# A planned DeltaNet and Fourier-mix kernel: every order drawn anew on a changed plan, integer additions on GpSimd in halves, second table loaded in four

## The chip, the cores and the metric

The kernel runs on one core of a Trainium2 chip. The metric is the device time of one execution in microseconds (us); the time before is the median of three runs.

## The reference: what is computed

For each of 4 batches and 8 heads, the first block walks through 768 tokens of width 48 with a 48x48 state (DeltaNet). The second block takes the heads joined to rows of 384, adds the real part of a Fourier transform over tokens and features, normalises each row and applies a two-layer MLP with 1536 hidden columns.

```python
for t in range(S):
    kt, vt, bt = k_n[:, :, t], v[:, :, t], beta[:, :, t, None]
    y[:, :, t] = einsum('bhd,bhde->bhe', q[:, :, t], state)
    v_old = einsum('bhde,bhd->bhe', state, kt)
    state = state + bt[..., None] * einsum('bhd,bhe->bhde', kt, vt - v_old)
...
u = x + real(fft(fft(x, axis=1), axis=2))
un = (u - mean(u)) / sqrt(var(u) + 1e-6)
out = u + maximum(un @ w_ch1, 0) @ w_ch2
```

The two weight matrices arrive as 64-bit floats. The kernel makes 32-bit floats of them with integer operations.

## The kernel before, in words

**Units and rounds.** Each batch is cut into 6 units of 128 tokens, 24 units in all. Units are prepared in rounds: round 0 has 2, round 1 has 4 (these six are batch 0), and six later rounds have 3 each (`SIZES`). Preparing a unit means loading its k, q and v, turning k and q on TensorE against the identity (L565), forming blocks of k times k (`keys`, `gram`), and inverting triangular blocks on VectorE. Rounds 0 and 1 invert in `begin16`/`invert16` (L897 transposes, L957/L963 multiply and add), later ones in `begin`/`invert` (L853, L868, L1046/L1051, L1063). A chain of state steps then runs through the units of a batch, `chain0` for batch 0 and `step` for the others.

**Mixing and MLP.** When a batch's last unit is done, `mixing` folds its rows on VectorE (L1451), multiplies by the sine and cosine tables `tab` (batch 0 with the first table, later batches with a smaller second one, both in the same tile) and `ft`, normalises (L1604 to L1629), and runs the MLP (L562 with `R`, `w` names, ReLU in L1695). Matmuls all go through the helper at L562, turns through L565, evictions mostly through L571 (ScalarE) or L573/L575 (VectorE).

**Weights.** `weights` brings the two matrices in 18 pieces of 128x512. For each piece: two DMAs or four into a stage buffer (L613), a ScalarE absolute value (L2015), a VectorE clamp (L2018), a ScalarE scaled copy of the low words (L2021), a VectorE shift (L2026), one GpSimd integer addition of 512 columns (L2031), and a VectorE step that puts the sign back (L2034) and needs the addition.

**What sets the order.** Every operation above is entered in a `Plan` with a cost for each engine that may run it, what it reads and writes, a priority and for some a due time. `Plan.schedule` walks a modelled clock and picks for each engine what to start next; `Plan.issue` then writes the instructions out in just that order, so the order on each engine, the DMA queue SP included, is fixed at build time. It rests on:

- due times of the batches and of the MLP: `M00`, `M0`, `MP`, `MX`, `MN`, `MA`, `MT`, `MD` (used in `due_a`, `due_m`, `normed`), and offsets `IV`, `IV1` (inversions) and `WP` (weights). Due times go back from each operation to what it needs. The smallest `pr` goes first;
- `KEYS`: for each 64 operations a number that shifts their priorities by up to 2.5 either way (`shift`);
- `LIM`, `LIM2`: how many of the 8 PSUM banks each class of work may hold before and after `TSW`;
- `START`, `LATER`: settings of the picking rule before and after `TSW`;
- the port rule: while GpSimd is in an operation marked `port=True`, no VectorE operation so marked is started, and the other way round;
- a model of transfers: 0.45 for an issue, `RATE` 190 KB/us, 2 us to land;
- a model of the fetch of TensorE's instructions (`fetch`: `LAND`, `LAND2`, `HOLDUP` and others) and of TensorE's clock (`speed`: costs are doubled while a window of `WIN` 3.413 us has held too few columns).

**Filler matmuls.** Where TensorE has nothing to start, the plan puts matmuls whose result nobody reads (`idle`). Before `E2` = 5.0 one filler is a group of six small ones (L2265), later it is one 256-column matmul or two half-size ones (L2272). In addition, between 20 and `D1` fillers go ahead of ordinary work whenever the last `SPANW` us held fewer than `TARGET` columns per us (`light`). `Plan.issue` writes a filler that starts before 1.5 three times (`OPEN` = 3).

**Hot operations.** `P.hot` marks operations that TensorE's picking rule (`pick`) takes ahead of all else when the mark is 1, and that are only spared by some filters when it is 2. Before, `chain0` has 2 (`HOTC`).

Of the kernel before, what the change touches and what calls it, by code (L numbers as in the profile page):

```python
# [10 lines left out]
I32 = mybir.dt.int32  # L11
U32 = mybir.dt.uint32
AX = mybir.AxisListType
ALU = mybir.AluOpType
# [4 lines left out]


SHIFT, PART = 5.0, 64
KEYS = [0, 196, 0, 882, 0, 533, 747, 349, 300, 92, 0, 631, 0, 118, 229, 329, 112, 81, 189, 0, 488, 857, 205, 426, 209, 734, 514, 433, 0, 264, 416, 0, 634, 135, 91, 0, 140, 556, 752, 279, 934, 886, 297, 564, 670, 480, 0, 737]
SIZES = 3, 3, 3, 3, 3, 3


# [7 lines left out]
class Op:  # L33
# [3 lines left out]

RATE = 190.0
WIN, WARM, COLD, CLOCK = 3.413, 600.0, 560.0, True
LOOK, EARLY = 1e9, 0.6403  # L40
FOLD, BY, SEQ, HOT, HOTPE, HOTPK, HOTG, NORM = 1, 1, 10, 5.6131, 8, 12, 1, 1
HOTC, PORT, E2, OPEN = 2, 1, 5.0, 3
GAP, HALF = 0.2477, 85.6671
LATE = -63.0868
PLOOK, PHOLD, PEND = 0.9458, 0.292, 163.9053
NHALF = 1
FORCE = -320.3215
BLOCK, LEAD, SEEK, LAND, LAND2, HOLDUP = 256, 60, 1.0, 2.0432, 1.8604, 1.0
PACE, PGAP, MOVED = 6.0, -0.4268, -0.7
PACED, AHEAD, SOON = 6.0, 1.6, 0.8  # L50
CUT, ROW = 256, 121
PLAIN, W1T = {(2, 2): (0, 1, 2, 3, 4, 5), (3, 2): (4, 5)}, 0.112
WF = 2, 2
TARGET, SPANW = 768.6683, 4.0822
E0, E1, D1 = 1.0, 10.0, 266.9663
TSW = 120.3811
# [6 lines left out]
LATER = {"SHARE": 0.4509, "HOLD": 0.168, "GAP2": 0.4292, "WAIT": 6.0709, "GATHER": 3.3164, "URGENT": -23.9166,  # L63
         "FIRST": 57.7347, "EV": 17.9188, "STAY": 0.2508, "CHAIN": 1.0}
START = {"SHARE": -0.4066, "HOLD": 0.343, "GAP2": 1.1196, "WAIT": 12.1835, "GATHER": 0.967, "URGENT": -81.5401,
         "FIRST": -86.5298, "EV": 4.7125, "STAY": 0.0, "CHAIN": 0.0}
LIM2 = {"state": 1, "sum": 4, "attn": 11, "mix": 4, "mlp": 4, "norm": 3, "win": 19}


T_F3, T_F2, T_PAIR = 0.36, 0.32, 0.52  # L70
# [3 lines left out]
class Plan:  # L74
# [116 lines left out]
    def schedule(self, pick, limits, switch, idle=None, span=()):  # L191
# [18 lines left out]
        moved, landed = MOVED, [0.0] * 8  # L210
# [9 lines left out]
        done, n, now = 0, len(ops), 0.0  # L220
        order, strict, last, self.hold = [], True, None, False
        self.order = order
        while done < n:
# [4 lines left out]
            for e in self.ENG:  # L228
                if free[e] > now + 1e-9:
                    continue  # L230
                best = None
# [8 lines left out]
                if e == "PE":  # L240
# [29 lines left out]
                    if (best is None and not low and now >= span[0][0] and  # L270
                            not any(o.ready["PE"] < now + (GAP if inside else K["GAP2"])
                                    for o in avail["PE"] if room(o))):
                        low = True
                    two = None
                    if low and best is None and idle:
                        m = "64" if mode == "64" and now < HALF else "128"
                        two = self.spare(now, m)
                    if two:
                        best = Op()
                        best.mode = m  # L280
                        best.i, best.fn, best.deps = -1, idle(two, m, now), set()
                        best.pr, best.lat, best.due, best.kb, best.col = 0.0, 0.0, 0.0, 0, 1150 if now < E2 else 512
                        best.ni = 24 if now < E2 else 8 if m == "64" else 4
                        best.engs, best.new, best.banks, best.succ = {"PE": 0.65 if now < E2 else 0.432}, [], [], []
                        for s in two:
                            slots[s] = now + 0.43
                elif cand:
# [20 lines left out]
                o = best  # L308
# [154 lines left out]
def kernel(  # L463
# [93 lines left out]
    def I(x):  # L557
        kp(x)
        P.ins = x.ins
# [23 lines left out]
    def t_pool(n):  # L583
        return 0.20 + n * 1.9e-3
# [25 lines left out]
    def dma(o, i, wr, pr, rd=(), kb=200, q="SP", cut=()):  # L610
        def fn(e):
            for x in cut or (slice(None),):
                I((nc.sync if q == "SP" else nc.scalar).dma_start(out=o[x], in_=i[x]))  # L613
        P.op({q: 0.45}, fn, rd, wr, pr, lat=2.0, kb=kb)

# [1367 lines left out]
    def weights(src, dst, rows, cols, where, pr, pieces=None):  # L1983
# [10 lines left out]
        for c0 in pieces:  # L1994
# [34 lines left out]
            def f4(e, cc=cc, rr=rr):  # L2029
                w = cc.bitcast(I32)  # L2030
                I(nc.gpsimd.tensor_tensor(w, w, rr.bitcast(I32), op=ALU.add))  # L2031

            def f6(e, cc=cc, hi=hi, c0=c0):
                I(nc.vector.scalar_tensor_tensor(  # L2034
# [223 lines left out]
    def idle(two, mode, now):  # L2258

        w = pack if now > E1 else p_[0]  # L2260

        def fn(e):
            if now < E2:
                for i in range(6):
                    I(nc.tensor.matmul(pst[two[0]][0:64, 64 * i:64 * i + 64], lhsT=w[:, 0:64],  # L2265
                                       rhs=w[:, 64:128], start=True, stop=True,
                                       skip_group_check=True))
                return
            for i in range(2 if mode == "64" else 1):
                x = slice(64 * i, 64 * i + 64) if mode == "64" else slice(0, 128)  # L2270
                n = 64 if mode == "64" else 128
                I(nc.tensor.matmul(pst[two[0]][x, 0:256], lhsT=w[x, 0:n], rhs=w[x, 0:256],  # L2272
                                   start=True, stop=True, skip_group_check=True))
        return fn
# [36 lines left out]
```

## Time and profile before

| what | value |
|---|---|
| median of three runs | 636.96 us (636.93 to 637.67) |
| the profiled execution | 636.25 us, span 634.4 us |
| TensorE busy (matmuls) | 616.8 us, 97% |
| VectorE busy | 512.4 us, 81% |
| ScalarE busy | 269.2 us, 42% |
| GpSimd busy | 35.9 us, 6% |
| instructions | 23099 |
| data moved by DMA | 32.02 MB |

The span runs from the first instruction to the last; the profiled execution's time is 1.85 us more. The tables of the profile name engines PE (TensorE), PEld (its weight loads), DVE (VectorE), ACT (ScalarE), POOL (GpSimd), SP (SyncE, here the queue of transfers). A name ending in q is the engine's sequencer. In a row of the timeline the first number is the start, the second the length, in us, and in brackets is how long the engine stood idle and who ended that; in the chain of waits the second number is the time that the step cost the chain. "Busy" counts any time with a matmul in flight, also when few columns flow, and it counts fillers.

### The profile page before, as it was taken

Reading aid. Unit: us, or ns where it says so; the run is one execution under the profiler, and the core shown is the slowest. Engines: PE = TensorE matmul, PEld = TensorE weight load, DVE = VectorE, ACT = ScalarE, POOL = GpSimd, SP = SyncE. Lnnn points to the kernel's source line nnn. Section 1 sums busy time; section 2 is a strip of 40 time slices with the busy share of each in tenths; the row PEclk is TensorE's granted clock in tenths of the full one; section 3 lists DMA queues with packets and bytes.
Section 4 is the critical chain, followed back from the end, with each engine's and each line's share of the span. In section 5 each row is a group of like instructions: output and inputs, shape, how many; then the busy total and the mean of one; then the engine's idle time right before and its main releaser. Section 6 shows DMA issues by size and latency. Waiting matters only on the chain.

```text
span 634.4 us, 23099 instructions
## 1 busy us (share of the span) xinstructions
PE 616.8 (97%) x9924; PEld 505.2 (80%) x9924; DVE 512.4 (81%) x1524; ACT 269.2 (42%) x791; POOL 35.9 (6%) x42
## 2 busy tenths in 40 slices
PE   8999899999899999999999999999999999999998
PEld 7788888777678777777787788677777889999997
DVE  6999899999995799999945999999666463856573
ACT  5698667531347533425364254253441141322110
POOL 3104311320000000000000000000000000000000
PEclk9999999999999999999999999999999999999999
DMA  8765565300124220001321200000000000000000
GB/s 168 191 193 130 136 134 157 100 3 25 26 42 104 41 53 2 25 3 34 83 54 39 65 14 1 25 3 2 5 28 2 0 26 1 26 1 27 1 26 26
DMA packets 85440, 32.02 MB, mean 50 GB/s; under 512 B 75992, under 2 KB 80825, under 8 KB 85337
## 3 DMA queue, kind: packets, MB, share of 16 engines
q1 hardware_dynamic: 85145, 30.31, 19.3%
q8 instruction: 78, 1.28, 0.8%
q10 hardware_dynamic: 192, 0.23, 0.1%
q14 instruction: 25, 0.20, 0.1%
HBM read 25.81 MB, written 4.72 MB: 48 GB/s over the span
## 4 chain that ended last, share of the span: by engine, by line
PE 73%; DVE 20%; ACT 3%; issue 3%; DMA 1%; DVEq 0%; SPq 0%; ACTq 0%
PE pp L562 69%; DVE tmp L1046 3%; DVE rr L1051 3%; PE pp L565 3%; ACT us L571 1%; DVE w L2034 1%; PE pp L2265 1%; DVE w L2018 1%; DVE gd L807 1%; PE pp L2272 1%; DVE R L1451 1%; DVE us L784 1%; DVE rr L897 1%; DVE rr L853 1%; DVE tmp L957 1%
## 5 line engine op out<-in xcount | busy, mean ns | idle before, releaser
L562 PE MATMUL pp<-R,w 128*128 128x256 f32 (+1 forms) x832 | 182.6, 367 | 0.2 <-DVE us L784 0.2
L562 PEld LDWEIGHTS pp<-R,w 128*128 128x128 f32 x832 | 145.2, 190 | 19.3 <-issue 0.4
L562 PE MATMUL pp<-w,R 128*128 128x384 f32 x384 | 134.8, 494 | 0.0
L571 ACT ACTIVATE us<-pp 32x128 f32<-32x128 f32 (+3 forms) x240 | 75.8, 348 | 80.6 <-PE pp L562 61.1
L562 PEld LDWEIGHTS pp<-w,R 128*128 128x128 f32 x384 | 69.9, 190 | 40.7 <-issue 0.2
L562 PE MATMUL pp<-us 64*64 64x64 f32 (+4 forms) x2784 | 68.4, 229 | 3.1 <-issue 1.6
L1695 ACT ACTIVATE R<-pp 128x512 f32<-128x512 f32 x48 | 28.7, 597 | 98.2 <-PE pp L562 87.6
L562 PEld LDWEIGHTS pp<-us 64*64 64x64 f32 (+2 forms) x2784 | 57.5, 131 | 9.2 <-issue 3.5
L1046 DVE TENSOR_TENSOR tmp<-rr 128x30 f32<-128x30 f32 (+9 forms) x180 | 57.7, 328 | 2.0
L1051 DVE TENSOR_TENSOR rr<-rr,tmp 128x108 f32<-128x108 f32 (+9 forms) x180 | 56.6, 323 | 2.0
L562 PEld LDWEIGHTS pp<-u,us 64*64 64x64 f32 (+1 forms) x1472 | 36.2, 130 | 15.8 <-issue 8.2
L562 PE MATMUL pp<-u,us 64*64 64x48 f32 (+2 forms) x1472 | 42.2, 216 | 0.9 <-DVE mv L573 0.6
L1870 DVE TENSOR_TENSOR us<-us,pp 128x256 f32<-128x256 f32 x64 | 26.7, 419 | 12.1 <-ACT us L571 9.8
L571 ACT ACTIVATE R<-pp 128x192 f32<-128x192 f32 (+6 forms) x82 | 22.8, 336 | 31.6 <-PE pp L565 19.6
L1360 DVE TENSOR_TENSOR u<-u,pp 64x192 f32<-64x192 f32 x66 | 22.3, 349 | 17.1 <-PE pp L562 14.9
L1826 DVE TENSOR_TENSOR gd<-us 128x128 f32<-128x128 f32 x48 | 11.8, 288 | 23.4 <-ACT us L1902 15.2
L571 ACT ACTIVATE x<-pp 64x192 f32<-64x192 f32 (+1 forms) x78 | 24.0, 322 | 14.9 <-PE pp L562 12.4
L562 PE MATMUL pp<-st,us 48*64 48x48 f32 (+1 forms) x1232 | 28.1, 221 | 2.0 <-DVE tmp L1046 0.7
L562 PEld LDWEIGHTS pp<-st,us 48*64 48x64 f32 x1232 | 23.7, 134 | 7.6 <-issue 3.9
L571 ACT ACTIVATE u<-pp 64x192 f32<-64x192 f32 (+1 forms) x71 | 23.1, 326 | 13.3 <-PE pp L562 8.9
L562 PE MATMUL pp<-us,gd 128*128 128x192 f32 x144 | 27.8, 327 | 0.0
L1426 DVE TENSOR_TENSOR x<-x,pp 64x192 f32<-64x192 f32 x66 | 23.2, 352 | 4.6 <-PE pp L562 2.8
(173 smaller groups left out, 959.5 us busy)
## 6 DMA issues: line engine op xcount, KB each, us to landing
out_dram<-x SPq DMA_DIRECT2D x11, 384.0 KB
us<-in_k_dram SPq DMA_DIRECT2D x16, 192.0 KB
us<-in_q_dram SPq DMA_DIRECT2D x16, 192.0 KB
us<-in_v_dram SPq DMA_DIRECT2D x16, 192.0 KB
x<-in_moe_w_ch_dram SPq DMA_DIRECT2D x12, 242.0 KB
R<-in_moe_w_ch_dram SPq DMA_DIRECT2D x6, 256.0 KB
us<-in_k_dram SPq DMA_DIRECT2D x8, 181.5 KB
us<-in_v_dram SPq DMA_DIRECT2D x8, 181.5 KB
```

Source lines behind the costliest of these rows:

```text
L562: I(nc.tensor.matmul(o, lhsT=lhsT, rhs=rhs, start=start, stop=stop, skip_group_check=True))
L565: I(nc.tensor.matmul(o, lhsT=src, rhs=ident[p0:p0 + n, p0:p0 + n], is_transpose=True, start=start, stop=True, skip_group_check=True))
L571: I(nc.scalar.activation(o, i, ACT.Copy, **({} if scale is None else {"scale": scale})))
L784: I(nc.vector.tensor_tensor(z.LT.rearrange(hs, s=2)[:, s], bk()[:, 0], m_su[:, None, :].broadcast_to([128, NJ, 64]), op=ALU.mult))
L807: I(nc.vector.scalar_tensor_tensor(w[0], w[1], (m1, m0)[s], w[2], op0=ALU.mult, op1=ALU.add))
L1046: I(eng(e).tensor_tensor(T_, R[:, :, j + 1:32, j:j + 1].broadcast_to([128, ns, n, j]), R[:, :, j:j + 1, 0:j].broadcast_to([128, ns, n, j]) ...
L1051: I(eng(e).tensor_tensor(R[:, :, j + 1:32, 0:j], R[:, :, j + 1:32, 0:j], T_, op=ALU.add))
L1360: I(nc.vector.tensor_tensor(U[:, s], U[:, s], psum(b1[s])[a, s0:s1].rearrange("p (j d) -> p j d", d=D), op=ALU.subtract))
L1426: I(nc.vector.tensor_tensor(w, w, v, op=ALU.add))
L1695: I(nc.scalar.activation(o, s, ACT.Relu))
L1826: vec(128, lambda e, j=j, i0=i0, i1=i1, op=op: I(nc.vector.tensor_tensor(s(j), i0, i1, op=op)), [aH] + rd, [aS(j)], pr - P.ev)
L1870: vec(256, lambda e: I(nc.vector.tensor_tensor(o, i0(), i1(), op=ALU.add)), [], [aH] + list(wr), pr - P.ev, use=n)
```

## The change

The code changes in seven places, and all of the plan's numbers are replaced.

1. **Opening.** The threefold writing of the first filler is gone. Until the modelled time 5.3 (`OPEN`) TensorE is given fillers alone, from 1.0 on, each a group of six at a cost of 0.7 (doubled while the modelled clock is low). The later kind of filler is counted as 600 columns, not 512.
2. **Transfers.** A transfer's landing after 16 us is planned 1.0 us later (`SLACK`). An issue costs 0.75 for over 50 KB and 0.3 for less.
3. **Integer additions.** L2031 becomes two of 256 columns.
4. **Second table.** Its one DMA of 641 KB becomes four column blocks.
5. **`HOTC`** goes from 2 to 1, `HOTG` from 1 to 7 (the last pair of normalised rows gets the mark too).
6. **Forced fillers.** `TARGET` goes from 768.7 columns per us over 4.08 us to 110.2 over 1.55 us, `D1` from 267 to 157.
7. **Due times, keys, bank limits, fetch times** are all new, so the order on every engine is another.

```diff
-KEYS = [0, 196, 0, 882, ...]
+KEYS = [5, 715, 997, 791, ...]
-WIN ... LOOK, EARLY = 1e9, 0.6403
+LOOK, EARLY = 1e9, -56.6693
-HOTC, PORT, E2, OPEN = 2, 1, 5.0, 3
+HOTC, PORT, E2 = 1, 1, 5.0
-BLOCK, LEAD, SEEK, LAND, LAND2, HOLDUP = 256, 60, 1.0, 2.0432, 1.8604, 1.0
+BLOCK, LEAD, SEEK, LAND, LAND2, HOLDUP = 256, 60, 1.0, 2.2969, 1.7353, 1.0
+OPEN, SLACK = 5.3, 1.0
-TARGET, SPANW = 768.6683, 4.0822
+TARGET, SPANW = 110.1955, 1.5494
-E0, E1, D1 = 1.0, 10.0, 266.9663
+E0, E1, D1 = 1.0, 10.0, 156.9524
-LIM = {"state": 1, "sum": 15, "attn": 6, "mix": 15, "mlp": 11, "norm": 8, "win": 4}
-NW, IV, IV1, WP = 9, 7.4111, 10.4756, -12.4024
-M00 = 96.1793
-M0, MP, MX, MN, MA, MT, MD = 80.4991, 115.1443, 13.2967, 35.8474, 19.0779, 5.7128, 8.8744
+LIM = {"state": 1, "sum": 36, "attn": 12, "mix": 6, "mlp": 16, "norm": 2, "win": 4}
+NW, IV, IV1, WP = 8, 10.1887, 18.6311, -4.1803
+M00 = 69.1361
+M0, MP, MX, MN, MA, MT, MD = 68.5709, 117.666, 17.0826, 39.7315, 19.3597, 6.0685, 9.8539
...
+                    if now < OPEN:
+                        best, low, wait = None, now >= E0, True
...
-                    landed.append(moved + o.lat - (SOON if now < 4.0 else 0.0))
+                    landed.append(moved + o.lat + (SLACK if now > 16.0 else -SOON if now < 4.0 else 0.0))
...
-            for _ in range(OPEN if o.i < 0 and o.start < E0 + 0.5 else 1):
-                o.fn(o.eng)
+            o.fn(o.eng)
...
-        P.op({q: 0.45}, fn, rd, wr, pr, lat=2.0, kb=kb)
+        P.op({q: 0.75 if kb > 50 else 0.3}, fn, rd, wr, pr, lat=2.0, kb=kb)
...
-            P.op({"POOL": t_pool(n) + 0.2}, f4, [a0], [ac], pr, lat=LP, port=True)
+            for h in (0, n // 2):
+                ...
+                P.op({"POOL": 0.73}, f4(h), [A(w0[0], w0[1] + 2 * h, w0[1] + 2 * h + n)],
+                     [A(dst, c0 + h, c0 + h + n // 2)], pr, lat=LP, port=True)
...
-    dma(tab[:, 0:20 * (N6 - 1) + 2], cn["tab6"].ap(), [A(tab, 0, 1)], 0, kb=656)
+    quart = 5 * (N6 - 1)
+    for x in range(4):
+        c = slice(quart * x, quart * (x + 1) + (2 if x == 3 else 0))
+        dma(tab[:, c], cn["tab6"].ap()[:, c], [A(tab, 0, 1, 32 * x, 32 * x + 32)], 0, kb=164)
```

More of the change, by code (lines that the diff above doesn't have):

```diff
@@ L39 @@
 WIN, WARM, COLD, CLOCK = 3.413, 600.0, 560.0, True
-LOOK, EARLY = 1e9, 0.6403
-FOLD, BY, SEQ, HOT, HOTPE, HOTPK, HOTG, NORM = 1, 1, 10, 5.6131, 8, 12, 1, 1
-HOTC, PORT, E2, OPEN = 2, 1, 5.0, 3
-GAP, HALF = 0.2477, 85.6671
-LATE = -63.0868
-PLOOK, PHOLD, PEND = 0.9458, 0.292, 163.9053
-NHALF = 1
-FORCE = -320.3215
-BLOCK, LEAD, SEEK, LAND, LAND2, HOLDUP = 256, 60, 1.0, 2.0432, 1.8604, 1.0
-PACE, PGAP, MOVED = 6.0, -0.4268, -0.7
-PACED, AHEAD, SOON = 6.0, 1.6, 0.8
+LOOK, EARLY = 1e9, -56.6693
+FOLD, BY, SEQ, HOT, HOTPE, HOTPK, HOTG, NORM = 1, 1, 12, 5.5524, 5, 13, 7, 1
+HOTC, PORT, E2 = 1, 1, 5.0
+GAP, HALF = 0.2162, 60.2432
+LATE = -132.6752
+PLOOK, PHOLD, PEND = -5.6692, 0.308, 137.4887
+NHALF = 1
+FORCE = -2.3955
+BLOCK, LEAD, SEEK, LAND, LAND2, HOLDUP = 256, 60, 1.0, 2.2969, 1.7353, 1.0
+PACE, PGAP, MOVED = 6.0, -0.4266, -0.7
+PACED, AHEAD, SOON = 6.0, 1.0, 0.8
+OPEN, SLACK = 5.3, 1.0
 CUT, ROW = 256, 121
@@ L53 @@
 WF = 2, 2
-TARGET, SPANW = 768.6683, 4.0822
-E0, E1, D1 = 1.0, 10.0, 266.9663
-TSW = 120.3811
-LIM = {"state": 1, "sum": 15, "attn": 6, "mix": 15, "mlp": 11, "norm": 8, "win": 4}
-NW, IV, IV1, WP = 9, 7.4111, 10.4756, -12.4024
-M00 = 96.1793
-M0, MP, MX, MN, MA, MT, MD = 80.4991, 115.1443, 13.2967, 35.8474, 19.0779, 5.7128, 8.8744
[L63 to L67, printed above, removed]
+TARGET, SPANW = 110.1955, 1.5494
+E0, E1, D1 = 1.0, 10.0, 156.9524
+TSW = 120.835
+LIM = {"state": 1, "sum": 36, "attn": 12, "mix": 6, "mlp": 16, "norm": 2, "win": 4}
+NW, IV, IV1, WP = 8, 10.1887, 18.6311, -4.1803
+M00 = 69.1361
+M0, MP, MX, MN, MA, MT, MD = 68.5709, 117.666, 17.0826, 39.7315, 19.3597, 6.0685, 9.8539
+LATER = {"SHARE": 0.4054, "HOLD": 0.163, "GAP2": 0.4686, "WAIT": 4.4142, "GATHER": 1.0248, "URGENT": -28.396,
+         "FIRST": 57.2003, "EV": 19.1605, "STAY": 0.1775, "CHAIN": 1.0}
+START = {"SHARE": -0.3965, "HOLD": 0.332, "GAP2": 0.3371, "WAIT": 38.0349, "GATHER": 1.1976, "URGENT": -53.5033,
+         "FIRST": -126.5871, "EV": 8.6017, "STAY": 0.0, "CHAIN": 0.0}
+LIM2 = {"state": 1, "sum": 4, "attn": 17, "mix": 5, "mlp": 6, "norm": 5, "win": 18}
 T_F3, T_F2, T_PAIR = 0.36, 0.32, 0.52
@@ L281, in schedule @@
                         best.i, best.fn, best.deps = -1, idle(two, m, now), set()
-                        best.pr, best.lat, best.due, best.kb, best.col = 0.0, 0.0, 0.0, 0, 1150 if now < E2 else 512
-                        best.ni = 24 if now < E2 else 8 if m == "64" else 4
-                        best.engs, best.new, best.banks, best.succ = {"PE": 0.65 if now < E2 else 0.432}, [], [], []
+                        best.pr, best.lat, best.due, best.kb, best.col = 0.0, 0.0, 0.0, 0, 1010 if now < OPEN else 600
+                        best.ni = 24 if now < OPEN else 8 if m == "64" else 4
+                        best.engs, best.new, best.banks, best.succ = {"PE": 0.7 if now < OPEN else 0.432}, [], [], []
                         for s in two:
@@ L2027, in f3, with f4 @@
                                           op1=ALU.logical_shift_right))
-            def f4(e, cc=cc, rr=rr):
-                w = cc.bitcast(I32)
-                I(nc.gpsimd.tensor_tensor(w, w, rr.bitcast(I32), op=ALU.add))
+            def f4(h, cc=cc, rr=rr):
+                w, r = cc[:, h:h + n // 2].bitcast(I32), rr[:, h:h + n // 2].bitcast(I32)
+                return lambda e: I(nc.gpsimd.tensor_tensor(w, w, r, op=ALU.add))
             def f6(e, cc=cc, hi=hi, c0=c0):
@@ L2262, in fn @@
         def fn(e):
-            if now < E2:
+            if now < OPEN:
                 for i in range(6):
```

6 lines of the change are left out of this document (5 added, 1 removed).

## The prediction

> **What bounds the kernel now.** I read the stages first (busy time by stretch), then the chain of waits, then the timeline at its long steps. In the table by stretch the columns are length, then busy time of PE, PEld, DVE, ACT and POOL with instructions in brackets.
>
> ```profile
> 0.00:10.00 10.00, 8.82 (x170) 8.24 (x174) 4.57 (x36) 2.66 (x6) 5.75 (x12) 1.00 0.90 184
> 10.00:45.00 35.00, 33.49 (x888) 26.07 (x890) 34.13 (x117) 28.55 (x92) 2.18 (x7) 1.00 0.74 185
> 45.00:108.00 63.00, 58.08 (x1582) 53.30 (x1573) 57.83 (x161) 45.05 (x127) 16.67 (x13) 1.00 0.57 145
> 108.00:163.60 55.60, 55.54 (x346) 40.93 (x344) 54.97 (x159) 19.97 (x52) 10.04 (x6) 1.00 0.12 39
> 163.60:182.00 18.40, 15.38 (x480) 12.22 (x480) 17.33 (x51) 9.92 (x32) 0.31 (x1) 1.00 0.13 26
> 182.00:634.40 452.40, 445.45 (x6482) 364.45 (x6482) 343.55 (x1004) 163.06 (x486) 0.94 (x3) 1.00 0.11 26
> ```
>
> From 182 on TensorE has work nearly always: 6.95 us without a matmul in 452. Before 108 its busy share means little, since fillers are in it:
>
> ```profile
> L2272 PE MATMUL pp<-pack 64*64 64x256 f32 (+1 forms) x124 | 18.9, 382 | 0.4 <-DVE eo L1604 0.4
> ```
>
> These 18.9 us and the 5.45 of the opening (below) are such fillers, nearly all before 108. What holds the first 182 us is VectorE (34.13 of 35, 57.83 of 63, 54.97 of 55.6), with GpSimd and the transfers beside it. Real TensorE work is fixed in amount, so a new order wins by getting the VectorE chain through to 108, where the first MLP starts, and to 182 sooner. After 182 it can win at most the 6.95 us, of which some 3 are the output's way out.
>
> **The change part by part. The opening.** The chain of waits at the start:
>
> ```profile
> 1.18 4.61 PE pp L2265 x48
> 5.79 0.39 PE pp L565 x8
> 6.18 0.49 PE pp L2076 x6
> 6.67 0.84 PE pp L2265 x12
> 7.51 0.39 PE pp L565 x8
> ...
> 11.52 1.99 DVE rr L897
> ```
>
> No transfer stands on this chain: the first turn (L565) waits for eight filler groups in front of it, the second for two more. How early its data was there is bounded by the transfers; in the rate row each number is 0.25 us:
>
> ```profile
> GB/s 0 0 0 0 0 0 0 137 100 208 232 272 336 271 313 257 239 228 257 237 189 214 164 198 182 224 250 216 181 138 204 217 217 241 259 257 275 218 214 222
> ...
> us<-in_k_dram SPq DMA_DIRECT2D x6, 192.0 KB
> ...
> pack<-k_pack ACTq DMA_DIRECT2D x1, 130.0 KB
> x<-in_beta_dram ACTq DMA_DIRECT2D x1, 96.0 KB
> ```
>
> Adding the numbers times 0.25 us, 610 KB (pack, beta and two k tiles) had moved by 4.4 us. So the first two turns could go up to 1.3 us (5.72 less 4.4) and then 0.84 us sooner. The changed plan doubles the filler's 0.7 while its clock is low, so groups start at 1.0, 2.4, 3.8 and 5.2: four of six matmuls, all ahead of real work. By the cold pace of the first 48 (4.61/48 = 96 ns each) they end near 3.5, before the data. Gain on the path: up to 2.1 us. Against it stands the clock, seen in the fillers' own lengths (minimum/median/maximum ns; first and last start):
>
> ```profile
> L2265 PE MATMUL pp<-pb x12: 314/314/315, 2.7 to 3.9; 128*64 128x64 f32 x12
> L2265 PE MATMUL pp<-pb x14: 222/222/222, 4.8 to 5.6; 128*64 128x64 f32 x14
> ```
>
> The array gets fast after 3 us of filling (the granted clock in the table by stretch says 1.00 and doesn't show this). With only 2.3 us of it, the two turns may run at 96 instead of 49 ns each (0.39/8): 16 x 0.047 = 0.75 us back. I take 2.1 - 0.75 = **1.35 us gained**, ends 0 and 2.1. The Trainium skill, "TensorE: Matmul & The Clock Gate", Part 1, says that the gate opens after a window of about 3.4 us with sustained work; the trace agrees (slow to 3.9, fast from 4.8), and by that rule four groups alone don't open it. What it would do here is the cold opening among the rivals.
>
> **Integer additions in halves.** While GpSimd adds, a VectorE operation that starts in that time can stand still:
>
> ```profile
> 66.46 1.31 POOL L2031 TENSOR_TENSOR w<-w,x 128x512 int32<-128x512 int32 x1
> 66.58 1.74 DVE L2034 SCALAR_TENSOR_TENSOR w<-R,w 128x512 int32<-128x512 int32 x1
> ...
> 134.45 0.68 DVE L2034 SCALAR_TENSOR_TENSOR w<-ws,w 128x512 int32<-128x512 int32 x1
> ```
>
> 1.74 instead of 0.68: 1.06 us lost. The same befalls one L2018 (maximum in the row below) and the L1451 and L1611 of these rows, and three steps of the chain:
>
> ```profile
> L2018 DVE TENSOR_SCALAR w<-w x18: 405/418/1525, 45.6 to 129.7; 128x512 f32<-128x512 f32 x18
> ```
>
> ```profile
> 90.31 1.71 DVE L1451 TENSOR_TENSOR eo<-x 128x191 f32<-128x191 f32 x2
> ...
> 112.71 1.58 DVE L1611 TENSOR_TENSOR x<-x,eo 128x384 f32<-128x384 f32 x1
> ```
>
> ```profile
> 122.81 1.19 DVE gb L872
> ...
> 126.93 1.26 DVE tmp L1046
> ...
> 131.61 1.30 DVE gd L807
> ```
>
> Seven such meetings at some 1.06 are 7.4 us of a full engine, three before 108 and four after. A half lasts half as long, so one meeting should cost some 0.5; but there are twice as many halves to meet. I take 0.4 saved each (0 and 1.06 are the ends). Before 108: 3 x 0.4 = **1.2 us**. After 108 TensorE has MLP work until 163.6, so VectorE's four savings (1.6) count only in the hole behind it:
>
> ```profile
> 165.48 0.22 PE L562 MATMUL pp<-t,us 64*32 64x32 f32 x2 [1.88 <-DVE t L1079]
> ```
>
> I take half of this 1.88, **0.9 us** (ends 0 and 1.88); a second engine, ScalarE with its evictions, is late next. What starting 18 more instructions costs GpSimd no row shows; it lies between 0 and another half of 1.31 us each, 12 us at most on an engine busy 16.67 of 63 and 10.04 of 55.6 us: I take 0, since its queue is mostly empty. Without that cover a piece's L2034 would come up to 0.65 us later.
>
> **Transfers planned later.** A late transfer holds up an engine's whole queue. ScalarE's one long case:
>
> ```profile
> 93.05 0.70 ACT L2015 ACTIVATE w<-x 128x512 f32<-128x512 f32 x1 [1.50 <-DMA x<-in_moe_w_ch_dram]
> ```
>
> TensorE had table matmuls then. I take 0 (ends: 1.5 gained; 1.5 lost where a reader that needn't have waited is now placed later). The new issue costs lie under the transfers of 192 KB, about 1 us each at this rate: 0.
>
> **Second table in four.** Three more issues on SP, which stand ahead of the loads of later k, q, v and the outputs:
>
> ```profile
> 104.78 0.44 SPq L613 DMA_DIRECT2D tab<-k_tab  x1
> ```
>
> ```profile
> 245.47 5.08 PE L562 MATMUL pp<-tab,R 128*97 128x65 f32 x48 [0.43 <-DVE R L1451]
> ```
>
> 3 x 0.44 = 1.3 us of an idle queue, and 140 us until the first reader, which waits for VectorE: 0, and 1.3 if the cover were gone.
>
> **The rest of the order** (keys, bank limits, `HOTC`, forced fillers): no row shows the new order. At best it shuts what idles after 182 (6.95 less 3, so 4 us), at worst it opens as much again. I take 0.
>
> **Sum:** 1.35 + 1.2 + 0.9 = 3.45 us. The profiled execution took 636.25 (span 634.4 and 1.85 around it), so 632.8; the median of the runs shown is 0.71 above that execution: **633.5 us**. Its own range, from the ends of opening and halves at half weight, is 631 to 635.6.
>
> **The rivals.** *Weights late (slower).* The due times of batch 0 come 27.0 us earlier (`M00` 96.2 to 69.1), those of the MLP 11.9 (`M0`), while `WP` puts the weights 8.2 back: weights lose some 23 us of rank against batch 0 on VectorE and ScalarE. Now they are already just in time:
>
> ```profile
> 108.06 4.26 PE L562 MATMUL pp<-R,w 128*128 128x256 f32 x19
> ```
>
> The last piece is ready at 135.13 (L2034 at 134.45, above), 27.1 us after the first MLP matmul. The first pair of units needs it after 10 steps of 12 matmuls, at 4.26/19 each 26.9 us. It decides as soon as the last piece comes later than that: four more pieces left over at the MLP's start, at 0.68 + 0.42 for L2034 and L2018 and, for the shift of the same size, 0.42 again, are 6.1 us of wait; less the 3.45 gained, 2.7 lost: **639.7**. For it: VectorE has no room before 163. Against: MLP steps of the next pair need only the earlier pieces and can fill the hole.
>
> *Gains that don't arrive.* ScalarE (28.55 of 35 us before 45) is late right behind VectorE; the opening's 2.1 us is eaten by the next transfer, and halves meet VectorE twice as often: 636.96 less at most 0.5, **637.0**. That the new order does nothing of what its parts say comes out here too.
>
> *Cold opening.* If the gate stays low for the first units' keys as well, their 64 matmuls (2 x 0.62 us now) take 1.24 us more: of 1.35 stays 0.1, **634.7**. The Trainium skill's page named above speaks for it.
>
> *A lucky order.* Opening 2.1, halves 0.55 before each of three meetings (1.65), the hole shut (1.88) and 2 of the 4 us after 182: 7.6, **629.4**.
>
> **How the numbers follow.** Forecast 0.38; weights late 0.34; no gain 0.13; cold opening 0.09; lucky order 0.06. A measurement of this kernel tells some 0.2% (1.27 us) from no change: faster is below 635.7, slower above 638.2. So faster 0.53, same 0.13, slower 0.34. The weights' wait may also be half as long again (641.2); the range leaves out that upper end and the best lucky orders: 630.0 to 640.5.
>
> **What would show it.** Right: 24 L2265 matmuls, the first turn before 5 and L897 near 10; no VectorE operation stretched by over 0.7 us beside L2031; the first `R,w` matmul near 105; the hole at 163 under 1 us. Wrong: TensorE waiting for L2034 or for L2031 in the MLP of batch 0; L897 still at 11.5, and turns of 0.75 us; over 7 us without a matmul after 182; transfers ending TensorE's waits. If the first MLP starts earlier but the end does not follow, the sum's step from VectorE's chain to the end is what failed.

## The result and the profile after

| | before | after |
|---|---|---|
| median (lowest to highest) of five runs on one chip | 637.67 us (636.93 to 639.06) | 643.06 us (641.15 to 644.33) |
| profiled execution, span | 636.25 us, 634.4 us | 643.50 us, 641.7 us |
| ratio after to before | | 1.0076, 95% interval 1.0048 to 1.0104 |

The kernel became slower, by 5.4 us of the medians. The forecast was 633.5 us.

Line numbers after the change are two to eleven higher: L562 is now L564, L2031 is L2033, L2034 is L2036, L2265 is L2276, L2272 is L2283, L897 is L899. First the table by stretch of the changed kernel, cut as that of before (length, busy PE, PEld, DVE, ACT, POOL, granted clock, DMA share, GB/s):

```profile
0.00:10.00 10.00, 8.13 (x190) 7.67 (x194) 4.68 (x37) 3.57 (x8) 5.61 (x11) 1.00 0.87 178
10.00:45.00 35.00, 32.82 (x766) 26.04 (x757) 32.14 (x110) 26.37 (x81) 2.18 (x7) 0.95 0.63 150
...
182.00:641.70 459.70, 447.90 (x6667) 368.09 (x6665) 346.29 (x1017) 166.46 (x498) 0.93 (x3) 0.99 0.11 26
```

Read the last row against that of before (452.40 long, 445.45 busy). In these two executions the whole loss lies there: 459.70 less 452.40 is 7.3 us, as much as the spans differ. It comes in two kinds. Time without a matmul went from 6.95 to 11.8 us, and time with matmuls from 445.45 to 447.90. The matmuls left at 182 are more (6667 against 6482), but of a different mix: counted by shape, 192 more small ones and six more of the filler's, and 15 fewer of 384 columns. At the pace of the trace's dense runs that is about nothing (3.5 + 1.3 - 4.8 us), so I take both kernels to be equally far at 182. The row of 10 to 45 shows a clock of 0.95: it fell for 3.4 us from 14.4 on, right behind a pause of 2.00 us. That cost lies ahead of 182 and is not in the 7.3 us; it comes up again below.

What TensorE waited for, first after, then before (in total, times, longest):

```profile
PE pp L564 <- issue: 13.4, 14, 2.0
PE pp L564 <- DVE t L1081: 0.8, 1, 0.8
```

```profile
PE pp L562 <- issue: 3.8, 6, 1.2
PE pp L562 <- DVE t L1079: 1.9, 1, 1.9
```

"Issue" is time in which the engine waits for nothing that the profile shows. I read it as data that is there and instructions that are not; the experiments test this. It rose by 9.6 us. Of the 14 pauses, five lie after 190 (1.49 and 1.52 at 198.6 and 202.4, then 1.33, 0.93 and 1.14), 6.41 us together; before had 2.75 there. Here is the place of the longest two, in the chain of waits, and the stretches around it:

```profile
197.07 1.57 PE pp L564 x92
200.13 2.30 PE pp L564 x127
202.43 1.52 issue
203.95 14.94 PE pp L564 x285
```

```profile
198.20:201.60 3.40, 1.91 (x121) 1.69 (x117) 1.90 (x6) 1.56 (x5) 0.00 (x0) 1.00 0.60 118
201.60:205.00 3.40, 1.88 (x82) 1.61 (x79) 0.34 (x1) 2.96 (x11) 0.00 (x0) 0.57 0.35 65
205.00:208.40 3.40, 3.40 (x102) 3.40 (x98) 1.53 (x5) 1.09 (x5) 0.00 (x0) 0.50 0.01 2
208.40:211.80 3.40, 3.40 (x15) 1.93 (x8) 0.91 (x3) 2.16 (x8) 0.00 (x0) 0.50 0.31 63
211.80:215.20 3.40, 3.40 (x117) 2.48 (x116) 1.25 (x4) 0.38 (x2) 0.00 (x0) 0.92 0.05 8
```

Between one MLP step that ends at 193.5 and the next at 208.6 stand 18 small operations in a row, 512 matmuls of the trace; in the old order the longest such run after 100 us is 13, with 368. TensorE works 1.9 of 3.4 us there, twice, and then its granted clock is 0.50 for 10.2 us (202.1 to 212.3). Two rows show it in the matmuls themselves (minimum/median/maximum ns), the first at half clock, the second just behind it:

```profile
L564 PE MATMUL pp<-us x64: 303/360/471, 204.9 to 208.3; 48*64 48x128 f32 x32, 64*64 64x48 f32 x32
L564 PE MATMUL pp<-us x64: 218/218/253, 213.9 to 218.7; 64*64 64x64 f32 x32, 64*64 64x48 f32 x32
```

VectorE works 0.34 to 1.90 us of each 3.4 in these rows, so it is not what holds TensorE up, and nothing covers the loss. Busy time times the missing share of the clock (1.88 x 0.43 + 3.40 x 0.50 twice + 3.40 x 0.08) gives 4.5 us; the longer pauses after 190 give another 3.66. That is 8.2 against the 7.3 to be explained, so this estimate is 0.9 too high; I did not take the difference apart.

### The profile page after: what moved, and what is told of

The parts are those of the page before. It is cut to its first block, busy times and chain, and to the rows that moved or that the text cites. A ratio compares the mean times of both kernels' runs of the same rounds, so it can differ in the third digit from the quotient of the medians.

```text
span 641.7 us, 23137 instructions
## 1 busy us (share of the span) xinstructions
PE 618.2 (96%) x9914; PEld 507.4 (79%) x9914; DVE 512.5 (80%) x1526; ACT 268.3 (42%) x790; POOL 38.3 (6%) x59
## 4 chain that ended last, share of the span: by engine, by line
PE 69%; DVE 23%; issue 4%; DMA 2%; ACT 1%; SPq 1%; DVEq 0%; ACTq 0%
PE pp L564 65%; DVE tmp L1048 4%; DVE rr L1053 4%; PE pp L2283 3%; PE pp L567 2%; DVE R L1453 2%; DVE rr L855 1%; DVE us L786 1%; DVE pm L1453 1%; DVE gd L809 1%; DVE w L2036 1%; DVE us L817 1%; DMA ws<-in_moe_w_ch_dram 1%; DVE eo L1453 1%; DVE x L1428 1%
## 5 line engine op out<-in xcount | busy, mean ns | idle before, releaser
L564 PE MATMUL pp<-R,w 128*128 128x256 f32 (+1 forms) x832 | 182.8, 367 | 0.0
L564 PEld LDWEIGHTS pp<-R,w 128*128 128x128 f32 x832 | 145.5, 190 | 19.0 <-issue 0.2
L564 PE MATMUL pp<-w,R 128*128 128x384 f32 x384 | 136.6, 501 | 0.3 <-DVE w L2036 0.3
L564 PEld LDWEIGHTS pp<-w,R 128*128 128x128 f32 x384 | 70.9, 192 | 42.9 <-issue 1.4
L564 PE MATMUL pp<-us 64*64 64x64 f32 (+4 forms) x2784 | 68.2, 233 | 4.5 <-issue 4.5
L564 PEld LDWEIGHTS pp<-us 64*64 64x64 f32 (+2 forms) x2784 | 58.2, 134 | 9.9 <-issue 6.6
L1053 DVE TENSOR_TENSOR rr<-rr,tmp 128x30 f32<-128x30 f32 (+12 forms) x180 | 57.8, 331 | 2.1
L1048 DVE TENSOR_TENSOR tmp<-rr 128x234 f32<-128x234 f32 (+13 forms) x180 | 57.3, 328 | 1.9
L564 PEld LDWEIGHTS pp<-u,us 64*64 64x64 f32 (+1 forms) x1472 | 36.1, 130 | 17.7 <-issue 14.0
L564 PE MATMUL pp<-u,us 64*64 64x48 f32 (+2 forms) x1472 | 42.4, 217 | 2.8 <-issue 2.8
L1391 DVE TENSOR_TENSOR st<-st,pp 128x192 f32<-128x192 f32 x30 | 10.5, 351 | 30.5 <-PE pp L564 30.4
L564 PE MATMUL pp<-st,us 48*64 48x48 f32 (+1 forms) x1232 | 29.2, 223 | 3.6 <-issue 2.5
L564 PEld LDWEIGHTS pp<-st,us 48*64 48x64 f32 x1232 | 24.7, 136 | 9.2 <-issue 7.6
L1828 DVE TENSOR_TENSOR gd<-us 128x128 f32<-128x128 f32 x48 | 11.8, 287 | 25.1 <-ACT us L1904 17.2
L573 ACT ACTIVATE R<-pp 128x192 f32<-128x192 f32 (+7 forms) x82 | 22.3, 335 | 20.1 <-PE pp L564 10.9
L564 PE MATMUL pp<-us,gd 128*128 128x192 f32 x144 | 27.4, 327 | 0.0
```

What stands on the lines that cost most here:

```text
L564: I(nc.tensor.matmul(o, lhsT=lhsT, rhs=rhs, start=start, stop=stop, skip_group_check=True))
L573: I(nc.scalar.activation(o, i, ACT.Copy, **({} if scale is None else {"scale": scale})))
L1048: I(eng(e).tensor_tensor(T_, R[:, :, j + 1:32, j:j + 1].broadcast_to([128, ns, n, j]), R[:, :, j:j + 1, 0:j].broadcast_to([128, ns, n, j]) ...
L1053: I(eng(e).tensor_tensor(R[:, :, j + 1:32, 0:j], R[:, :, j + 1:32, 0:j], T_, op=ALU.add))
L1391: I(nc.vector.tensor_tensor(sn[:, s0:s1], so[:, s0:s1], psum(b2)[:, s0:s1], op=ALU.add))
L1828: vec(128, lambda e, j=j, i0=i0, i1=i1, op=op: I(nc.vector.tensor_tensor(s(j), i0, i1, op=op)), [aH] + rd, [aS(j)], pr - P.ev)
```

## The experiments

**Theory.** The new order puts small matmuls side by side so densely that instructions don't come fast enough; TensorE pauses, does too little in some stretch of about 3.4 us, and its clock is halved. **Rivals:** the pauses come from loads that run at the same time (the second table and tiles of k in the way of the instructions); or a part of the change costs by itself (halves, opening, table in four), and the order is innocent.

**Loads moved out of the run.** The changed order kept; five loads go to behind operation 1085.

```diff
     P.pace()
+    by = {o.i: o for o in P.order}
+    for i in (1521, 1543, 1522, 1544, 1750):
+        by[i].after = by[1083]
...
+    at = P.order.index(by[1085]) + 1
+    P.order[at:at] = k
     P.issue()
```

> The changed kernel with every engine's order kept, but for five loads of k, q and v that stood in the transfer queue at 198.0 to 201.0: they now wait for a state step that ended at 205.4. Theory F: the change lost its time where TensorE ran out of instructions (1.49 us at 198.6, 1.52 us at 202.4) and its clock then fell to half for 10.24 us. F-collision: these loads made the instruction fetch late, so without them both pauses fall under 0.5 us each, the clock stays at 1.00 and the time goes from 643.1 to some 637. F-density: the run of small matmuls alone outpaces the fetch; the pauses and the clock's fall stay, 643. Rival O: the time was lost along VectorE's chain and with the late weights; 643, and if the pauses vanish the end does not move.

Measured: 639.71 us (636.65 to 641.48, 12 runs), ratio to before 1.0025 (1.0006 to 1.0044); profiled span 637.1. The timeline at the same place, and its stretches:

```profile
198.81 0.49 PE L564 MATMUL pp<-us 64*64 64x48 f32 x17 [0.79 <-issue]
202.63 0.19 PE L564 MATMUL pp<-pb,t 64*32 64x32 f32 x1 [1.61 <-issue]
```

```profile
198.20:201.60 3.40, 2.21 (x127) 1.94 (x128) 1.83 (x6) 2.31 (x8) 0.00 (x0) 1.00 0.02 5
201.60:205.00 3.40, 2.37 (x125) 2.33 (x125) 0.94 (x3) 2.58 (x10) 0.00 (x0) 1.00 0.13 26
205.00:208.40 3.40, 2.33 (x24) 1.49 (x17) 0.81 (x3) 2.08 (x8) 0.00 (x0) 1.00 0.79 159
```

The loads are gone (DMA share 0.02 instead of 0.60) and the pauses stay, so loads don't make them; a third of 1.07 comes at 206.3. In sum they are 3.47 us here, against 3.01 with the loads: the first is shorter (0.79 for 1.49), the second is not (1.61 for 1.52). But TensorE works 2.2 to 2.4 us of each 3.4 instead of 1.9, and the clock holds at 1.00. Compared at the same instructions, this run is 0.3 us ahead of the changed kernel before the place and 3.8 behind it, so the place gives 3.5 us; with pauses that are 0.46 longer, the halved clock cost about 4.0 there. (The rest of the spans' 4.6 comes later, where pauses are shorter.) The medians are 3.4 apart. The clock's fall is not gone from every execution: the mean clocks of the twelve are 0.989 to 1.000, those of the changed kernel's five 0.989 to 0.995. Neither theory was right alone.

**Wide matmuls put into the run.** The changed order kept; ahead of each of five operations between 198 and 205 TensorE does two more matmuls of 256 columns, ten in all, into banks that are overwritten.

```diff
+    for i in (1237, 1078, 1238, 1302, 1534):
+        ...
+            for _ in range(2):
+                nc.tensor.matmul(pst[s.slot][:, 0:256], lhsT=pack[:, 0:128], rhs=pack[:, 0:256],
+                                 start=True, stop=True, skip_group_check=True)
+            f(e)
```

> The changed kernel with its order kept; ten filler matmuls of 256 columns (two ahead of each of five operations between 198 and 205) are put into the same stretch, at some 0.43 us each 4.3 us of TensorE. Theory F: the array stays busy enough for the clock to hold at 1.00 where it fell to 0.5 for 10.24 us (5.1 us lost), and while a filler runs the fetch gets ahead, so part of the 3.0 us of pauses is filled: 643.1 - 5.1 + 4.3 - (0 to 3.0), that is 639 to 642. Rival O: the fillers are 4.3 us of additional work in a stretch where the clock does not matter: 643 to 647.

Measured: 641.58 us (638.92 to 644.43, 12 runs), ratio 1.0063 (1.0041 to 1.0084); profiled span 637.1, 4.6 us under the changed kernel's, at a granted clock of 0.999. That profile is the fastest of the twelve; by the medians the gain is 1.5 us, and the interval overlaps the changed kernel's.

```profile
198.20:201.60 3.40, 3.40 (x105) 2.50 (x103) 0.65 (x2) 1.03 (x4) 0.00 (x0) 1.00 0.47 93
201.60:205.00 3.40, 3.40 (x76) 2.54 (x76) 0.35 (x1) 3.03 (x11) 0.00 (x0) 1.00 0.03 7
205.00:208.40 3.40, 3.40 (x94) 2.68 (x87) 1.39 (x4) 2.14 (x8) 0.00 (x0) 1.00 0.20 38
```

Both pauses and the fall of the clock are gone, with the first loads still in place. Of the 4.6 us, though, only 1.7 belong to the place. The last MLP step in front of it, first in the changed kernel, then here, where every instruction up to it is the same:

```profile
190.65 2.86 PE L564 MATMUL pp<-R,w 128*128 128x256 f32 x12
188.42 2.86 PE L564 MATMUL pp<-R,w 128*128 128x256 f32 x12
```

This execution is 2.2 us ahead before the first wide matmul, and 3.9 behind the place. Of these 2.2, 1.3 arise between 14 and 22 us, where its clock did not fall; the changed kernel's did, and so did that of the run with the loads moved. The changed kernel there:

```profile
14.30:17.80 3.50, 3.50 (x43) 2.29 (x43) 2.81 (x10) 2.24 (x9) 0.00 (x0) 0.51 0.76 151
```

The 1.7 agree with the medians' 1.5. The ten fillers are 4.4 us of work (20 matmuls of the trace at some 0.22), and the kernel is not slower for them: adding work was free, since it stood where TensorE would have waited or crawled.

**Instructions by themselves, one quarter of the array.** Nothing of the reference is computed here; the output is zeros.

In order, as the program counts its matmuls:

```text
40 wide | 640 small | 40 wide | 640 small, a wide one after every 32 | 40 wide
| 640 small beside eight loads of 144 KB | 40 wide
```

> No part of the reference is computed (the output is zeros): TensorE alone does 40 wide matmuls (128x128 by 256 columns), then 640 small ones (64x64 by 48 columns) without a break, 40 wide, 640 small with a wide one after every 32, 40 wide, 640 small while SP loads eight tiles of 147 KB, 40 wide. Theory of density: a block of 256 instructions holds 128 of the matmuls of the trace with their weight loads, which a dense run uses up in 2.5 us, and the next block comes only after 3.6 to 4.4 us; so the first run of small ones shows a pause of 1 to 2 us about every 128, with no transfer of data in sight, and the clock falls to half in it; with wide ones in between the pauses are shorter by about the 0.9 us that the wide ones last. Rival, collision with loads: no pauses in the first two runs, pauses in the third alone. The third run also tells what loads add.

Measured: 500.04 us, span 498.2, mean clock 0.589. An fp32 matmul stands twice in the trace.

```profile
20.40:27.20 6.80, 6.80 (x100) 6.80 (x100) 0.00 (x0) 0.00 (x0) 0.84 0.00 0
27.20:153.30 126.10, 126.10 (x1184) 126.03 (x1182) 0.00 (x0) 0.00 (x0) 0.50 0.01 1
160.10:173.10 13.00, 13.00 (x61) 11.19 (x59) 0.00 (x0) 0.00 (x0) 1.00 0.00 0
```

The expectation failed: no pause at all, since matmuls that all use the same quarter take 104 ns each (133.0 us for 1280), so that 128 of them last 13 us, ample for the next block. But the clock is at 0.50 for as long as they last, with TensorE busy all the time (126.10 of 126.10), and at 1.00 in the wide ones. So the clock does not need a pause to fall: what counts is how much the array does, not how long TensorE is busy. The Trainium skill, "TensorE: Matmul & The Clock Gate", Part 1, ties the gate to how busy the array has been in a free-running window of about 3.4 us; the lengths of the falls agree (10.2 us is three such windows), but its "idle" has to be read as little work: here it falls without any idle time.

**The same round the four quarters**, as the kernel's small operations go, four side by side.

```diff
+        s, c = ((0, 0), (1, 1), (1, 0), (0, 1))[i % 4]
+        a = slice(64 * c, 64 * c + 64)
+        return nc.tensor.matmul(pst[2 * (n % 4) + c][64 * s:64 * s + 64, 64 * (i // 4):64 * (i // 4) + 48],
+                                lhsT=us[a, 64 * (i // 4):64 * (i // 4) + 64], rhs=us[a, 256:304],
+                                start=True, stop=True, skip_group_check=True)
```

> As the last run of TensorE alone (output zeros, nothing of the reference computed), but the small matmuls go round the four quarters of the array, as the kernel's do, so that four run side by side. There, in one quarter, they took 104 ns each at half clock and 61 at full, slower than instructions come, and no pause showed, though the clock fell. Here they should take about 20 ns each. Theory of density: pauses of 1 to 2 us about every 128 matmuls of the trace in the first run of small ones already, with no load in sight, so that 1280 take 40 to 50 us instead of 25; with two wide matmuls after each 64 the pauses shrink. Rival, collision with loads: 25 us without a pause in the first run, pauses in the third alone. On the clock: it falls to half in the run of small ones alone and comes back with the wide ones.

Measured: 183.53 us, span 181.7. The timeline of the first run, which has no loads, then part of the second, then the third, beside the loads:

```profile
21.30 4.17 PE L48 MATMUL pp<-us 64*64 64x48 f32 x271
26.43 2.08 PE L48 MATMUL pp<-us 64*64 64x48 f32 x128 [0.95 <-issue]
29.88 2.08 PE L48 MATMUL pp<-us 64*64 64x48 f32 x128 [1.38 <-issue]
33.61 2.08 PE L48 MATMUL pp<-us 64*64 64x48 f32 x128 [1.65 <-issue]
...
70.67 1.15 PE L48 MATMUL pp<-us 64*64 64x48 f32 x64
71.75 0.70 PE L53 MATMUL pp<-us 128*128 128x256 f32 x2
...
123.71 3.12 PE L48 MATMUL pp<-us 64*64 64x48 f32 x199
129.00 3.54 PE L48 MATMUL pp<-us 64*64 64x48 f32 x128 [2.17 <-issue]
135.75 3.47 PE L48 MATMUL pp<-us 64*64 64x48 f32 x128 [3.20 <-issue]
```

This is the pause, bare: exactly 128 matmuls and their 128 weight loads, 2.08 us of work (16 ns each), then 1.38 or 1.65 us of nothing, seven times over, with no load in sight (the first pause, with more in stock, is 0.95). A block of 256 instructions comes every 3.45 to 3.73 us and no faster. With one wide matmul after every 32 small ones a block lasts about that long, and one pause of 0.39 us is left in the whole second run. Beside loads the pauses grow to 2.2 and 3.2 us. The clock, by stretch of these three runs, and in a single stretch of the first:

```profile
21.30:53.20 31.90, 20.49 (x1281) 19.48 (x1280) 0.00 (x0) 0.00 (x0) 1.00 0.02 5
70.70:106.30 35.60, 35.09 (x1321) 27.44 (x1321) 0.00 (x0) 0.00 (x0) 1.00 0.02 5
123.70:163.40 39.70, 26.11 (x1282) 24.82 (x1281) 0.00 (x0) 0.00 (x0) 0.83 0.40 140
31.50:34.90 3.40, 1.75 (x120) 1.63 (x114) 0.00 (x0) 0.00 (x0) 1.00 0.02 5
```

Pauses alone leave it at 1.00, though half was expected (20.49 busy of 31.90); beside loads it falls to a mean of 0.83. In outline this is the changed kernel's place at 198: density makes the pauses, and with loads beside them the clock falls. It fits both runs above: without the loads the pauses stay and the clock holds; with wide matmuls neither comes. How the loads bring the clock down in the kernel is not shown. Here they lengthen the pauses; there the two pauses (1.49 and 1.52) are no longer than the bare ones here (1.38 and 1.65). Nor does busy time tell where the clock falls: 1.75 us of 3.4 held at 1.00 here, and 1.91 of 3.4 came just before the fall in the kernel, whose matmuls there are of other shapes. The Trainium skill, "Runtime: NRT & Kernel Launch", Instruction fetch mechanics, has the blocks of 256 instructions, and says that crossing into the next is mostly hidden, because instructions are dispatched more slowly than blocks are filled; the trace agrees on the block and disagrees on the rest, by 1.38 us in every 3.45.

**The additions in halves alone**, in the old order, and **whole again** in the new one.

```diff
             def f4(e, cc=cc, rr=rr):
-                w = cc.bitcast(I32)
-                I(nc.gpsimd.tensor_tensor(w, w, rr.bitcast(I32), op=ALU.add))
+                for h in (0, n // 2):
+                    w, r = cc[:, h:h + n // 2].bitcast(I32), rr[:, h:h + n // 2].bitcast(I32)
+                    I(nc.gpsimd.tensor_tensor(w, w, r, op=ALU.add))
```

> The kernel before with its order kept; each of the 18 integer additions on GpSimd is two instructions of 256 columns, one behind the other. The prediction's step: seven VectorE operations that stood still for some 1.06 us lose about 0.4 us less each, of which 2.1 us reach the end: 635.6 from 637.7. Rival: a VectorE operation held up waits for both halves, or meets the second one, so that nothing is saved: 637.7, with the same seven at 1.0 us and more.

Measured: 636.46 us (634.6 to 638.92, 12 runs), ratio 0.9978 (0.9960 to 0.9997). VectorE's busy time goes from 512.4 to 510.4. The halves gain 1.4 us (0.2 to 2.5).

```diff
             def f4(h, cc=cc, rr=rr):
-                w, r = cc[:, h:h + n // 2].bitcast(I32), rr[:, h:h + n // 2].bitcast(I32)
-                return lambda e: I(nc.gpsimd.tensor_tensor(w, w, r, op=ALU.add))
+                w, r = cc.bitcast(I32), rr.bitcast(I32)
+                return lambda e: h and I(nc.gpsimd.tensor_tensor(w, w, r, op=ALU.add))
```

> The changed kernel in its own order, with each integer addition whole again (one 512-column addition where its second half stood). In the old order the halves alone gave 1.1 to 1.4 us. If they help here as well, this run is slower than the changed kernel by 1 to 1.5 us, about 644. If the halves are part of the loss (twice as many meetings with VectorE), it comes back to 642 or below. Neither theory expects the pauses of TensorE at 198 to 206 or the fall of its clock to go.

Measured: ratio 1.0101 (1.0065 to 1.0137), median 644.29. It points to the slower side, as the gain from halves would have it, but the interval overlaps the changed kernel's, and the profiled run fell to half clock at about 100 to 114 us as well (mean 0.984), so the size of the difference says nothing on the additions. VectorE's busy time does: 514.8 us whole, 512.5 in halves. The halves are not the loss.

**The opening.** In the old order, the first filler issued once, then twice (the latter with the halves).

```diff
-            for _ in range(OPEN if o.i < 0 and o.start < E0 + 0.5 else 1):
-                o.fn(o.eng)
+            o.fn(o.eng)
```

> The kernel before with its order kept; the first filler is written once and not three times, so 24 fewer matmuls of the trace stand ahead of the first turn. The prediction's step: the first turn's data is there by 4.4, so the turn starts near 4.5 instead of 5.7 and the first transpose (L897) up to 1.3 us sooner; time 636.4 to 637.7. Rival: the turn waits for its k tile and starts at 5.4 or later, and with less filling the array stays slow for longer; nothing gained, or up to 1 us lost (638.7).

Measured: 640.61 us (634.49 to 644.11), ratio 1.0020 (0.9990 to 1.0049): the runs lie in two clumps, four of them about 635.5 and eight about 641. The opening of the profiled one, which is of the eight:

```profile
1.18 2.82 PE L2264 MATMUL pp<-pb 128*64 128x64 f32 x24 [1.18 <-DVE pb L687]
4.23 0.69 PE L564 MATMUL pp<-pack,us 64*128 64x64 f32 x8 [0.22 <-DMA us<-in_k_dram]
...
15.81 0.69 PE L564 MATMUL pp<-pack,us 64*128 64x64 f32 x8
```

The first turn comes 1.5 us earlier, as the prediction wanted it. But turns still take 0.69 at 15.81, where a warm one takes 0.46 (second turn of the next kernel, below), and VectorE's transposes, at 11.52 before, start at 12.50. With 24 matmuls the array stays slow in this execution. The four shorter runs may be those in which it got fast earlier; no profile shows one of them.

```diff
-HOTC, PORT, E2, OPEN = 2, 1, 5.0, 3
+HOTC, PORT, E2, OPEN = 2, 1, 5.0, 2
```

> The old order with the additions in two halves (636.46 so far), and the first filler issued twice instead of three times. If 36 matmuls are enough to open the clock, the first turn comes near 5.0 instead of 5.72 with its matmuls still at 49 ns, and the time is 635.8. If they are not enough, the array stays slow until about 20 us, as with 24, and the time is 636.5 to 640.

Measured: **634.48 us** (632.01 to 640.0, 12 runs), ratio 0.9969 (0.9950 to 0.9988), on a chip where before takes 636.75. This beats both kernels. Its opening:

```profile
1.18 4.10 PE L2266 MATMUL pp<-pb 128*64 128x64 f32 x36 [1.18 <-DVE pb L688]
5.21 0.69 PE L565 MATMUL pp<-pack,us 64*128 64x64 f32 x8
...
7.25 0.46 PE L565 MATMUL pp<-pack,us 64*128 64x64 f32 x8
```

36 matmuls are enough in this execution: only the first turn is slow, and the transposes start at 11.34. (One of the twelve runs, at 640.0, lies as far off as the eight above; it has no profile.) How much of the gain over the halves alone is the opening's, the two ratios can't tell (0.9969 against 0.9978, with intervals that overlap).

**All that can be put into the old order by hand:** the last kernel with the second table in four.

```diff
-    dma(tab[:, 0:20 * (N6 - 1) + 2], cn["tab6"].ap(), [A(tab, 0, 1)], 0, kb=656)
+    quart = 5 * (N6 - 1)
+    cut = [(slice(None), slice(quart * x, quart * (x + 1) + (2 if x == 3 else 0))) for x in range(4)]
+    dma(tab[:, 0:20 * (N6 - 1) + 2], cn["tab6"].ap(), [A(tab, 0, 1)], 0, kb=656, cut=cut)
```

> The old order with the parts that can be put into it by hand: additions in halves, the first filler issued twice, and the second table in four transfers. Without the table in four this was 634.48. If the parts are what they seemed and the new order alone loses, it is 634.0 to 635.0. If the table in four costs what its issues take (1.3 us), it is 635.8.

Measured: 635.81 us (634.38 to 638.5, 12 runs), ratio 0.9984 (0.9963 to 1.0006). Its interval overlaps the last kernel's, so whether the table in four costs 1.3 us or nothing stays open. Either way these parts in the old order are not slower than before: the loss of the change is in the new order and the settings that draw it.

**Another order from the same edits.** The changed kernel with the old list of keys, so that the planner draws a third order.

```diff
-KEYS = [5, 715, 997, 791, ...]
+KEYS = [0, 196, 0, 882, ...]
```

> The changed kernel with all its edits, but the list of keys of the old one: another order drawn from the same parts. If the parts decide (opening, halves, slack), the time stays within 1.5 us of the changed kernel's 643. If the draw of the order decides, it moves by much more than that, to either side, and the difference shows as pauses of TensorE, as time at half clock, or as waiting for VectorE before 182; the run of small operations near 200 is 13 long here instead of 18, so the clock should hold at that place.

Measured: 646.95 us (644.95 to 650.13, 4 runs), ratio 1.0181 (1.0156 to 1.0205). The clock holds in the profiled execution, as expected at a run of 13 (mean 0.999), and pauses are 8.5 us. The loss is elsewhere, as the last stretch shows:

```profile
182.00:643.20 461.20, 453.04 (x6726) 370.46 (x6725) 348.70 (x1015) 166.81 (x502) 0.94 (x3) 1.00 0.11 26
```

6726 matmuls are left at 182 instead of 6482, and the stretch is 8.8 us longer than before's, all of the difference of the spans. With nothing but keys changed the time moved by 6.7 us from the changed kernel, by the two ratios to before (1.0181 and 1.0076, on two chips): this draw is worth more than any part of the change that was measured by itself. What it consists of in this order was not taken apart further.

## Why the prediction was wrong

**The failed step** is "The rest of the order ... I take 0", with ends of 4 us either way. It measured +7.3 us behind 182: pauses for instructions (+3.7 after 190) and the clock that stood at half for 10.2 us where they met loads (about +4.0 by the run with the loads moved away); the two estimates together overshoot the 7.3 a little. The waits of before already had the row for it, "PE pp L562 <- issue: 3.8, 6, 1.2", and I did not ask what makes such a pause, nor when there would be more. The bound of 4 us upward came from mirroring what the old order had left to win, which is no bound on what a new one can lose. Of the signs of being wrong that I had named, one came in full: over 7 us without a matmul after 182 (11.8). Others came small: L899 at 12.16, 0.3 us of waiting for L2036, and 0.7 us for tiles of k in the opening.

**The 3.45 us ahead of 182** did not arrive either: in the profiled executions both kernels are equally far there. Part of that is one fall of the clock. The run with wide matmuls is the changed kernel up to 195; its clock did not fall at 14.4, and it is 2.2 us ahead from about 80 on. So the forecast's gains up to 182 were partly real, but an execution can lose them in its opening.

**Opening: 1.35 us gained, measured 0.6 us lost** (L899 at 12.16, before 11.52). I read "x48" as eight groups of six. An fp32 matmul stands twice in the trace, so they were four groups, and the changed plan's four are the same 48, not 24:

```profile
1.19 4.33 PE L2276 MATMUL pp<-pb 128*64 128x64 f32 x48 [1.19 <-DVE pb L690]
5.45 0.71 PE L567 MATMUL pp<-pack,us 64*128 64x64 f32 x16
...
8.57 2.09 PE L564 MATMUL pp<-us 48*64 48x64 f32 x126
12.66 0.74 PE L564 MATMUL pp<-us 48*64 48x64 f32 x34 [2.00 <-issue]
```

The first turn comes 0.27 us earlier, but then the keys' matmuls run 126 on end, and the first pause of 2 us falls into the chain. Had there been 24, the run with one filler shows that the *cold opening* can come true in full: in its profiled execution turns are slow from 4.2 to past 15.8 us, not just the two that I charged.

**Halves: right for one meeting, and in the old order.** 2.1 us forecast, 1.4 (0.2 to 2.5) measured there. In the new order additions meet VectorE more often, as the rival *gains that don't arrive* has it: 16 operations are stretched by over 0.2 us instead of 7 (11 with halves in the old order), by about 0.5 each, and VectorE is busy 512.5 us, against 512.4 before. No VectorE operation beside the additions is stretched by more than 0.58 (L2036 at most 1.26 against 0.68), near the 0.5 of the forecast, and the hole behind 163 shrank from 1.88 to 0.8, as said. But the first `R,w` matmul came at 108.01, not near 105: nothing brought the MLP forward.

**Weights late: the mechanism came, its price did not.** The last piece is ready at 145.8 instead of 135.1, 10.7 us later, as the loss of rank would have it:

```profile
145.11 0.68 DVE w L2036
```

TensorE waited 0.3 us once, at 139.4, for an earlier piece, and not for this one. MLP steps and table matmuls that needed only earlier pieces filled the time, the counter-argument that I had set against it. The time of this rival, 639.7, was nearer to the result than the forecast, but for another cause.

**Transfers:** not zero, though not by the way I looked: five loads, put elsewhere, were worth 3.4 us of the medians, and no row of waits names them.

## What to carry to other kernels

Count instructions per microsecond, not only busy time: in these runs TensorE got 256 per 3.5 us or so, and a run of small matmuls that uses them faster has a pause in every block. Spread wide matmuls between small ones (one of 256 columns after 32 small was enough), and keep loads out of dense runs, for the fall of the clock (about 4.0 us) cost more than the pauses beside it (3.0). A new order is not a zero in a sum: price it by its longest run of small operations, and where the planner draws it, by how far other draws of the same parts lie apart. And compare two profiles at the same instruction, not only by their spans: 2.2 of one run's 4.6 us had come from its opening, not from its edit.

## What the runs showed of the hardware

- A dense run of small matmuls round the four quarters of the array gets a block of 256 instructions every 3.45 to 3.73 us; beside loads of about 390 GB/s the pause grows from 1.38 or 1.65 to as much as 3.20 us.
- The clock falls to half with TensorE busy all the time, if the matmuls use one quarter of the array only (0.50 over 126 us); with four quarters in use 20.49 us busy of 31.90 kept it at 1.00.
- In the profiled executions 24 matmuls of 128x64 by 64 columns at the start leave the array slow until past 16 us and 36 do not, while the granted clock reads 1.000 in both; and the same 48 took 4.33 us in the profile of the changed kernel and 5.30 in that of the halves alone.
- A GpSimd addition of 512 columns stretches a VectorE operation that starts in it by about 1.06 us, one of 256 columns by at most 0.58 us.
